# A plan's order settled twice, late from its end and early from its front, with new operation lengths, and expert lists worked out at another place

## The chip, the cores and the metric

One Trainium2 chip, one core of it. The metric is the device time of one execution in microseconds (us); where several executions were timed, the median is taken. TensorE (PE) does the matmuls, VectorE (DVE), ScalarE (ACT) and GpSimd (POOL) the elementwise work, and SyncE (SP) issues nearly all DMAs. Each engine works through its own queue of instructions in order, and semaphores hold an instruction until what it needs is there.

## The reference

For each of 4 batches, 49 agents attend to 11456 keys, the queries attend to the agents, and each of the resulting 45824 rows of 128 goes through one of 8 experts (two layers, 128 to 1024 to 128), the one with the greatest gate logit:

```
a2k = softmax(agents @ k.T * scale);  agent_v = a2k @ v
x   = softmax(q @ agents.T * scale) @ agent_v
logits = x @ w_gate;  e = argmax(logits);  gate = softmax(logits)[e]
out = gate * (relu(x @ w1[e]) @ w2[e])
```

## The kernel before

Products are done in 16-bit pairs (a high part and what is left over), so that one product becomes two or three matmuls.

**Stages of a batch.** A batch is 9 units of 10 blocks of 128 rows. `k_ops` loads the keys, splits them (ACT the high part, POOL the low part, line 352), makes scores on PE and keeps the running maximum. `v_ops` subtracts the maximum, exponentiates and sums with the values. `dense_ops` folds the agents' values into the first layer's weights of the batch's commonest expert (`Md`, `Mq`). `q_head` makes the queries' weights (`rows`), stores them and loads them turned (`et`); `quads` copies a part of it four times (`etq`). `q_tail` makes gate logits, and `gate_ops` makes the gate of two units at a time.

**Dense tiles.** Every row goes through the commonest expert. A unit is three tiles (4, 4 and 2 blocks). A group is two first-layer results `hp` (lines 1207 and 1216), their two parts `hhi` (ACT, line 1236) and `hlo` (DVE, line 1241), and the second layer into `yp` (lines 1224, 1225, 1230). There are 180 such groups. PSUM has three `hp` buffers, so the next group's first layer waits until an `hlo` has been read out of the buffer that it wants. In `group_ops` each group's second layer comes behind the next group's first layer, so the order of groups on PE is fixed.

**Lists and the other experts.** `r_ops` works out, mostly on DVE, which rows of a batch belong to other experts (lines 1004 to 1190, tiles `big`, `idx`, `ohx`): it needs all gates of the batch, and `min_loads` and `min_tile` (fetch the rows, run them through their expert, scatter the result over the dense one) need it. There are 8, 5, 0 and 1 such tiles for the four batches. `ready` says behind which unit of a later batch they begin.

**The planner.** Every step is an `Op` with an engine, an assumed cost, a key (its due place, counted in dense blocks), and the steps and buffers that it depends on. `Plan.run` goes forward in time. Of all steps whose inputs and buffers are there it takes the one that can start first (within `SLACK`, the one with the smaller key), and it looks no more than `WINDOW` = 20 blocks ahead of the first step left. Loads share one modelled DMA path of 300 GB/s. The moment a step is taken, its instructions are emitted; the order in which they are taken is the order of each engine's queue.

Of the kernel before, what the change touches and what calls it, by code (L numbers as in the profile page):

```python
# [19 lines left out]
P = 128  # L20
# [23 lines left out]
SLACK0, SLACK = 0.1, 0.08  # L44
AHEAD0 = 40.0


# [38 lines left out]
class Plan:  # L86
# [18 lines left out]
    def run(self, window):  # L105
# [51 lines left out]
        while left:  # L157
# [47 lines left out]
def agent_attention_moe(ctx: ExitStack, tc: tile.TileContext, qT, kT, v, agT, wg, w1, w2, out):  # L205
# [128 lines left out]
    def split(src, key, hk, pool=False, rings=("chi", "clo"), parts_=1, early=False, lowcost=0):  # L334
        st = Rec()
        n = UC // parts_
        gf = [Gen("wf" if parts_ > 1 else "cf") for _ in range(parts_)]
        gh, gl = Gen(rings[0]), Gen(rings[1])
        st.f, st.ld = [], []

        def hi():
            st.hi = part(rings[0])
            for i, f in enumerate(st.f):
                nc.scalar.copy(st.hi[:, i * n:(i + 1) * n], f)  # L344

# [15 lines left out]
        o2 = PL.op("POOL" if pool else "DVE", ((lowcost or pol(UC) + 0.2) if pool else dve(UC)), lo, hk, [o1], new=[gl], use=gf + [gh])  # L361
        return st, [o1, o2], [gh, gl]

    def scores(t, st, sp, gs, key, pair=False):
# [3 lines left out]
        def mm():  # L368
            p = r.p = new_hp()[:, 0:UA].rearrange("p (j a) -> p j a", a=A) if pair else misc([P, UB, A])
            for j in range(UB):  # L370
# [3 lines left out]
                nc.tensor.matmul(p[:, j], l, t.a[:, 0], start=False, stop=True)  # L374
        o = PL.op("PE", 0.92, mm, key, sp + [t.o_a], new=[gm], use=gs)
        return r, o, gm
# [99 lines left out]
    def v_ops(t, key, pool=()):  # L476
# [8 lines left out]
        for u in range(NU):  # L485
# [60 lines left out]
            if not one and u + 1 not in firsts:  # L546
                continue
            oM.append(PL.op("PE", 1.14 * len(run) + 0.1, mm, k, wait_ + oM[-1:], new=[] if one and u else [gv],
                            use=gfs + [t.gS] + ([gv] if one and u else [])))
# [157 lines left out]
    def dense_ops(t, key):  # L707
# [44 lines left out]
        for h in range(2):  # L752
# [97 lines left out]
    def q_head(t, u, k, pool=True, low=True):  # L850
# [49 lines left out]
        o1 = PL.op("ACT", act(UA), ex, k, [o], use=[gx])  # L900
        o2 = PL.op("ACT", 0.13 + act(UA), ehi, k, [o1], new=[grow], use=[gx])
        o3 = PL.op("POOL" if pool else "DVE", (pol(UA) + 0.1 if pool else dve(UA)) + 0.1, elo, k, [o2], use=[gx, grow])
        o4 = PL.op("POOL" if pool else "DVE", (pol if pool else dve)(UB * R1), again, k, [o2], use=[grow])
        U.o_ag = o4
# [3 lines left out]
        if not (t.b == 0 and u == 0):  # L908
            U.o_et = [PL.op("SP", 2.3, turn, k, [o5], new=[gt], nbytes=2 * UC * P)]
            return  # L910
# [38 lines left out]
    def gate_ops(t, u0, u1, k):  # L949
# [24 lines left out]
        c = n * NE * 0.00107  # L974
        o = PL.op("DVE", 0.7 + 3 * c, g1, k, [U.o_lg for U in t.U[u0:u1]], new=[g3, g4], use=[t.glg, t.gsm])
        t.o_lg.append(o)
        o = PL.op("ACT", act(n * NE), g2, k, [o], use=[g3])
        o = PL.op("DVE", 0.85 + c, g3_, k, [o, t.o_sig], use=[g3, g4, t.gsig, t.gisc])
        for U in t.U[u0:u1]:
# [4 lines left out]
    def r_ops(t, key):  # L984
# [269 lines left out]
    def group_ops(i, first, last, items, nbk, l1, cost, y, gyp, deps, use, wdeps, wuse, w):  # L1254
# [6 lines left out]
        for p in range(np_):  # L1261
            def f1(p=p):
                x[p].hp = new_hp()
                l1(p, [z.hp for z in x[:p + 1]])
            o1.append(PL.op("PE", cost[p], f1, i - 2.2 + 0.05 * p, deps[p] + before + o1[-1:], new=[g[p][0]],
                            use=use + [g[q][0] for q in range(p)]))
# [13 lines left out]
        for p in range(np_):  # L1280
            def l2a(p=p):
                if first and p == 0:
                    y.yp = new_yp()
                layer2_hi(y.yp, w(), x[p].hi, items[p], nbk, first and p == 0)
            new = [gyp] if first and p == 0 else []
            G.l2.append(PL.op("PE", 0.9 if p else 1.0, l2a, i + 0.1 * p, [o4[p]] + wdeps + G.l2[-1:], new=new,
                              use=[g[p][1]] + wuse + ([] if new else [gyp])))
        for p in range(np_):
            def l2b(p=p):
                layer2_lo(y.yp, w(), x[p].lo, items[p], nbk, last and p == np_ - 1)  # L1290
            G.l2.append(PL.op("PE", 0.45, l2b, i + 0.3 + 0.1 * p, [o3[p]] + G.l2[-1:], use=[g[p][2], gyp] + wuse))
        groups.append(G)
# [9 lines left out]
    def quads(i, t, u):  # L1302
# [4 lines left out]
        def go():  # L1307
            U.etq = buf("etq", [P, UC], U16)
            for r in range(4):
                nc.sync.dma_start(U.etq[32 * r:32 * r + RC], U.et[0:RC])  # L1310
        U.o_q = PL.op("SP", 2.4, go, max(U.key + 3, i - 12) if U.key > -900 else U.key + 1, U.o_et, new=[U.gq], use=[U.gt], nbytes=4 * R2 * UC * 2)
        if t.b == 0 and u == 0:
            U.o_q.after += t.o_ld

    def dense_tile(i, t, u, j0, nbk):
# [10 lines left out]
        for q in range(ng):  # L1326
# [9 lines left out]
            o = group_ops(i + 2 * q, q == 0, q == ng - 1, items, nbk, l1, (0.43, 0.96), y, gyp,  # L1336
                          (U.o_et + (t.o_Md[q:q + 1] if nbk == 4 else t.o_Md), [U.o_q] + (t.o_Mq[q:q + 1] if nbk == 4 else t.o_Mq)), [U.gt, U.gq, t.gMd, t.gMq], [t.o_Wd], [t.gWd], lambda: t.Wd)
# [20 lines left out]
        o = PL.op("ACT", act(n), yo, e + 0.05, [o], new=[gyo], use=[gyp])  # L1358
        o = PL.op("POOL", pol(n) + 0.05 * (nbk // 2 - 1), mul, e + 0.08, [o, U.o_gate], use=[gyo, t.gisc])
        stores[b].append(PL.op("SP", 0.6, store, e + 0.1, [o], use=[gyo], nbytes=nbk * 65536))  # L1360

# [11 lines left out]
    def build_ops(i, e, key):  # L1373
# [22 lines left out]
        o = PL.op("ACT", act(F), hi, key + 2, [o], new=[gs], use=[gf])  # L1396
        o = PL.op("POOL", pol(F) + 0.1, lo, key + 2, [o], use=[gf, gs])
        o_parts[i].append(dma(None, None, P * F * 4, key + 2, [o], use=[gs], fn=lambda: nc.sync.dma_start(parts[i][e], r.s)))
# [48 lines left out]
    def min_loads(t, key):  # L1447
# [9 lines left out]
        def ix():  # L1457
# [7 lines left out]
            nc.vector.memset(r.rt, BIG_ID)  # L1465
        o = PL.op("SP", 1.0, ld, key, [t.o_lst], new=[gl], nbytes=t.cap * P * 8)
        oi = PL.op("DVE", 0.75, ix, key + 1, [o], new=[gi, r.grt, Gen("fx")], use=[gl])
        for j in range(t.cap):
# [27 lines left out]
            k = key + 2 + 4 * j  # L1496
            o = PL.op("POOL", 1.3, info, k, [oi, t.o_info], use=[r.grt, gi], nbytes=2000)
            o = PL.op("POOL", 1.5, get, k, [o] + t.o_eb, new=[ger], use=[r.grt], nbytes=33000)
            o = PL.op("PE", 0.06, tr, k + 1, [o], new=[gp], use=[ger])
# [5 lines left out]
    def min_tile(i, t, j):  # L1505
# [5 lines left out]
        def ld():  # L1511
            c.v, c.w = stage(t, ds(j, 1))
        o = PL.op("SP", 1.6, ld, i - 10, [t.o_tab] + o_parts[0] + o_parts[1], new=[gv, gw], nbytes=P * F * 8)
        y = Rec()
        gyp = Gen("yp")
        op = group_ops(i, True, True, [ONE], 1, lambda p, hps: layer1(hps[0], c.v, x.xt), (1.34,), y, gyp,
                       ([x.o, o],), [x.gxt, gv], [o], [gw], lambda: c.w)
# [8 lines left out]
        op = PL.op("ACT", 0.37, yo, i + 0.05, [op], new=[gyo], use=[gyp, r.grt])  # L1526
        PL.op("POOL", 1.3, sc, i + 0.1, [op] + stores[t.b], nbytes=65536, use=[gyo, r.grt])

# [4 lines left out]
    wait = []  # L1533
    ready = {(1, 2, 0): 0, (2, 2, 0): 1, (3, 2, 0): 2, (3, 8, 8): 3}
    n = gap = 0
# [39 lines left out]
    for t in BT:  # L1575
        f = first[t.b]
        for u in range(1 if t.b == 0 else 0, NU):
# [106 lines left out]
```

## Time and profile before

| | us |
|---|---|
| median of 3 runs | 1013.07 (1012.22 to 1019.42) |
| the profiled execution | 1009.59 |
| its span, first to last instruction | 1007.8 |
| mean granted TensorE clock | 0.972 |

The profile shows one execution. A busy share is the time in which an engine had an instruction under way; what ended the idle time before an instruction is found from semaphores. Times in windows count from the span's start.

### The profile page before, as it was taken

How to read it: one execution, taken by the hardware profiler on the slowest of the kernel's cores; microseconds unless marked ns; L12 is line 12 of the kernel's file. 1: busy time of each engine (PE TensorE's matmuls, PEld its weight loads, DVE VectorE, ACT ScalarE, POOL GpSimd, SP SyncE). 2: the span in 40 equal slices, each digit the busy share in tenths (PEclk: the TensorE clock that was granted, in tenths of full speed). 3: DMA queues.
4: the chain of work that ended last, by engine and by line, in shares of the span. 5: the costliest groups of instructions: out<-in, count | busy, mean ns of one | idle time of the engine just before them, and what ended most of it. 6: DMA issues, size and time to landing. Idle time of an engine off the chain costs nothing. (4 is left out here: it accounts for less than half of the span.)

```text
span 1007.8 us, 34309 instructions
## 1 busy us (share of the span) xinstructions
PE 928.7 (92%) x14812; PEld 756.5 (75%) x14812; DVE 713.1 (71%) x1088; ACT 656.6 (65%) x891; POOL 505.1 (50%) x710
## 2 busy tenths in 40 slices
PE   4799999999899999999998998999999999999794
PEld 4667877877577788787877887888877778777574
DVE  7666677678976666655899766665788876767852
ACT  6467988867586777654676777755667666655352
POOL 4124988555495888242355578842225433311231
PEclk8799999999799999999999999999999999999898
DMA  9547699963696476566344926683344535231211
GB/s 339 198 123 242 224 277 244 293 243 124 195 282 206 153 206 162 141 215 173 104 138 132 295 80 173 190 249 105 104 122 117 128 96 162 77 75 48 66 28 31
DMA packets 156575, 165.33 MB, mean 164 GB/s; under 512 B 60190, under 2 KB 130075, under 8 KB 156414
## 3 DMA queue, kind: packets, MB, share of 16 engines
q1 hardware_dynamic: 155070, 162.11, 53.9%
q8 instruction: 118, 1.93, 0.8%
q0 software_dynamic: 1344, 0.93, 0.4%
q14 instruction: 43, 0.35, 0.1%
HBM read 98.65 MB, written 45.50 MB: 143 GB/s over the span
## 5 line engine op out<-in xcount | busy, mean ns | idle before, releaser
L1241 DVE SCALAR_TENSOR_TENSOR hlo<-hp,hhi 128x1024 f16<-128x1024 f32 x374 | 445.3, 1218 | 189.4 <-ACT hhi L1236 183.8
L1236 ACT ACTIVATE hhi<-hp 128x1024 f16<-128x1024 f32 x374 | 367.7, 1022 | 159.7 <-PE hp L1216 151.7
L1224 PE MATMUL yp<-Wd,hhi 128*128 128x128 f16 x2880 | 352.3, 222 | 1.0 <-ACT yo L1341 0.6
L1225 PE MATMUL yp<-Wd,hhi 128*128 128x128 f16 x2880 | 350.7, 221 | 0.6 <-issue 0.6
L1224 PEld LDWEIGHTS <-hhi 128*128 128x128 f16 x2992 | 292.1, 99 | 34.4 <-issue 30.9
L1225 PEld LDWEIGHTS <-hhi 128*128 128x128 f16 x2992 | 296.0, 99 | 2.8 <-issue 2.3
L1346 POOL TENSOR_TENSOR yo<-yo,isc 128x256 f32<-128x256 f32 x180 | 112.8, 644 | 244.8 <-ACT yo L1341 206.6
L352 POOL TENSOR_TENSOR clo<-cf,chi 128x512 f16<-128x512 f32 x186 | 185.7, 1028 | 79.3 <-ACT chi L344 58.1
L1207 PE MATMUL hp<-et,Md 128*128 128x512 f16 (+1 forms) x864 | 195.8, 347 | 28.3 <-DVE hlo L1241 27.7
L1230 PE MATMUL yp<-Wd,hlo 128*128 128x128 f16 x2880 | 193.0, 219 | 3.4 <-DVE hlo L1241 2.2
L1230 PEld LDWEIGHTS <-hlo 128*128 128x128 f16 x2992 | 175.5, 98 | 5.7 <-issue 2.6
L1207 PEld LDWEIGHTS <-Md 128*128 128x128 f16 x864 | 75.3, 98 | 67.0 <-issue 37.4
L1341 ACT COPY yo<-yp 128x512 f32<-128x512 f32 (+1 forms) x108 | 55.7, 516 | 71.8 <-PE yp L1230 48.7
L344 ACT CAST chi<-cf 128x1280 f16<-128x1280 f32 x62 | 78.1, 1263 | 12.7 <-DMA cf<-in_qT 6.6
L885 POOL TENSOR_TENSOR rows<-xs,rows 128x245 f16<-128x245 f32 x72 | 44.6, 641 | 81.9 <-ACT rows L880 81.6
L1216 PE MATMUL hp<-etq,Mq 19*128 19x512 f16 (+1 forms) x864 | 73.2, 355 | 0.0
L1216 PEld LDWEIGHTS <-Mq 19*128 19x128 f16 x864 | 18.9, 91 | 71.0 <-issue 70.9
L374 PEld LDWEIGHTS <-clo 128*128 128x128 f16 x670 | 54.3, 97 | 4.4 <-POOL clo L352 4.1
L372 PE MATMUL misc<-a,chi 128*128 128x49 f16 x630 | 56.5, 185 | 1.1 <-DVE xt L1439 0.4
L374 PE MATMUL misc<-a,clo 128*128 128x49 f16 x630 | 56.2, 185 | 0.9 <-POOL clo L352 0.9
L373 PE MATMUL misc<-a,chi 128*128 128x49 f16 x630 | 56.2, 186 | 0.0
L372 PEld LDWEIGHTS <-chi 128*128 128x128 f16 x630 | 50.9, 96 | 6.6 <-issue 4.2
(263 smaller groups left out, 1102.7 us busy)
## 6 DMA issues: line engine op xcount, KB each, us to landing
cf<-in_kT SPq DMA_DIRECT2D x36, 640.0 KB
cf<-in_v SPq DMA_DIRECT2D x35, 640.0 KB
cf<-in_qT SPq DMA_DIRECT2D x35, 640.0 KB
out<-yo SPq DMA_DIRECT2D x72, 256.0 KB
eb<-rows SPq DMA_DIRECT2D x36, 320.0 KB
wf<-in_w SPq DMA_DIRECT2D x16, 512.0 KB
etq<-et SPq DMA_DIRECT2D x144, 50.0 KB
vst<-parts SPq DMA_DIRECT2D x14, 512.0 KB
```

The source lines that it names most:

```text
L344: nc.scalar.copy(st.hi[:, i * n:(i + 1) * n], f)
L352: (nc.gpsimd if pool else nc.vector).tensor_tensor(st.lo[:, o], f[:, d], st.hi[:, o], op=OP.subtract)
L372: nc.tensor.matmul(p[:, j], h, t.a[:, 0], start=True, stop=False)
L374: nc.tensor.matmul(p[:, j], l, t.a[:, 0], start=False, stop=True)
L1207: nc.tensor.matmul(hp[:, c:c + n], m[:, fb * P:(fb + 1) * P], e, start=c % 512 == 0, stop=False)
L1216: nc.tensor.matmul(hp[:, c:c + n], m[r:r + R2, fb * P:(fb + 1) * P], e[r:r + R2], start=False, stop=(c + n) % 512 == 0)
L1224: nc.tensor.matmul(y, h, w[:, fb * 256 + P:(fb + 1) * 256], start=first and j == 0 and i == 0, stop=False)
L1225: nc.tensor.matmul(y, h, w[:, fb * 256:fb * 256 + P], start=False, stop=False)
L1230: nc.tensor.matmul(yp[:, j * P:(j + 1) * P], lo[:, c + j * P:c + (j + 1) * P], w[:, fb * 256:fb * 256 + P], start=False, stop=last and j = ...
L1236: nc.scalar.activation(hi, hp, AF.Relu)
L1241: nc.vector.scalar_tensor_tensor(lo, hp, 0.0, hi, op0=OP.max, op1=OP.subtract)
L1346: nc.gpsimd.tensor_tensor(v3[:, j:j + 2], v3[:, j:j + 2], t.isc[:, k0 + j:k0 + j + 2, 1:2].bitcast(F32).to_broadcast([P, 2, P]), op=OP.mult)
```

## The change

1. `Plan.run` still chooses an order step by step, but emits nothing. A new function `settle` takes that order. It makes edges from the dependencies and from the order in which ring buffers are given out. Then three times over it places all steps from the end backwards, each as late as its users and its engine allow, and then from the front, the steps with the earliest late start first, each at the earliest free place on its engine, gaps between steps placed before included. Steps are emitted by these start times. `settle` has no window and no slack, and a DMA's landing is bytes / 300 GB/s + 4 us for each one by itself.
2. About 30 assumed costs are set anew.
3. The due places of the lists of batches 0 to 2 are moved back, beside the next batch's dense tiles and the following batch's keys and values, and the minor tiles of batches 0 and 1 begin three units later.

```diff
-            o.fn()
             left -= 1
...
-        self.order = order
-        return max(o.fin for o in order)
+        self.order = self.settle(order)
+        for o in self.order:
+            o.fn()
+        return self.span
+
+    def settle(self, order):
...
+        def edge(d, i, begin=False):
+            if at[d] != i:
+                o = order[i]
+                lag = -d.cost if begin else d.nbytes / 300e3 + 4.0 + d.more + 0.0 if d.nbytes else 0.0 if d.eng == o.eng else d.lat + 0.05
+                pred[i].append((at[d], lag))
+                succ[at[d]].append((i, lag))
+
+        for i, o in enumerate(order):
+            for d in o.deps:
+                edge(d, i)
+            for d in o.after:
+                edge(d, i, True)
+            for g in o.new:
+                r = rings.setdefault(g.ring, [])
+                k = RINGS.get(g.ring, 1)
+                if len(r) >= k:
+                    for u in r[len(r) - k][1].users:
+                        edge(u, i)
+                if r:
+                    edge(r[-1][0], i, True)
+                r.append((o, g))
...
+        def early(key):
+            t, busy = [0.0] * n, {}
+            for i in turns(pred, succ, key):
+                o = order[i]
+                x = max([t[p] + order[p].cost + lag for p, lag in pred[i]], default=0.0)
+                L = busy.setdefault(o.eng, [])
+                j = bisect_right(L, (x, 1e9))
+                if j:
+                    x = max(x, L[j - 1][1])
+                while j < len(L) and x + o.cost > L[j][0] + 1e-9:
+                    x = max(x, L[j][1])
+                    j += 1
+                L.insert(j, (x, x + o.cost))
+                t[i] = x
+            return t
...
+        t = [o.fin - o.cost for o in order]
+        for _ in range(ROUNDS):
+            ends = [x + o.cost for x, o in zip(t, order)]
+            t = early(late(ends, max(ends)))
+        self.span = max(x + o.cost for x, o in zip(t, order))
+        return [order[i] for i in turns(pred, succ, t)]
...
-        t.o_an = PL.op("DVE", 0.9, c7, k, [o3], new=[t.gan, t.gbm], use=[gp, t.gav] + ([ga] if one else []))
+        t.o_an = PL.op("DVE", 1.4, c7, k, [o3], new=[t.gan, t.gbm], use=[gp, t.gav] + ([ga] if one else []))
...
-        t.o_em = PL.op("DVE", 0.35, e2, k if t.b else 8, [o])
+        t.o_em = PL.op("DVE", 1.1, e2, k if t.b else 8, [o])
...
-                t.o_Mq.append(PL.op("SP", 2.0, spread, k, [o2], new=new, use=use + [gl], nbytes=4 * R2 * 1024))
+                t.o_Mq.append(PL.op("SP", 3.05, spread, k, [o2], new=new, use=use + [gl], nbytes=4 * R2 * 1024))
...
-        o8 = PL.op("DVE", dve(n8), a8, k, [o7], new=[Gsf], use=[Gb])
+        o8 = PL.op("DVE", 1.5, a8, k, [o7], new=[Gsf], use=[Gb])
...
-            o10 = PL.op("DVE", 0.6, a10, k, [t.o_idx], new=[Ghl], use=[t.gidx])
+            o10 = PL.op("DVE", 1.4, a10, k, [t.o_idx], new=[Ghl], use=[t.gidx])
...
-        U.o_q = PL.op("SP", 2.4, go, max(U.key + 3, i - 12) if U.key > -900 else U.key + 1, U.o_et, new=[U.gq], use=[U.gt], nbytes=4 * R2 * UC * 2)
+        U.o_q = PL.op("SP", 3.15, go, max(U.key + 3, i - 12) if U.key > -900 else U.key + 1, U.o_et, new=[U.gq], use=[U.gt], nbytes=4 * R2 * UC * 2)
...
-    ready = {(1, 2, 0): 0, (2, 2, 0): 1, (3, 2, 0): 2, (3, 8, 8): 3}
+    ready = {(1, 5, 0): 0, (2, 5, 0): 1, (3, 2, 0): 2, (3, 8, 8): 3}
...
-                r_ops(t, Keys(k + 10, k + (42 if t.b < 3 else 22), 12))
+                r_ops(t, Keys(k + 10, k + 22, 12) if t.b == 3 else Keys(f + 92, f + 128, 12))
```

No instruction is added or removed; the order in each queue is what changes.

## Rows read from the trace of the kernel before

**Rows 1.** The page: busy time, share of the span and instructions of each engine.
```profile
PE 928.7 (92%) x14812; PEld 756.5 (75%) x14812; DVE 713.1 (71%) x1088; ACT 656.6 (65%) x891; POOL 505.1 (50%) x710
```

**Rows 2.** Windows: stretch, its length, each engine's busy time, granted clock, DMA share.
```profile
0.00:45.00 45.00, 25.97 (x484) 23.79 (x484) 29.19 (x65) 25.61 (x34) 11.44 (x24) 0.81 0.83 294
45.00:215.00 170.00, 162.69 (x2656) 131.34 (x2656) 118.25 (x187) 129.97 (x176) 110.74 (x153) 0.99 0.76 231
215.00:285.00 70.00, 60.37 (x814) 46.79 (x813) 59.60 (x90) 49.55 (x64) 40.23 (x44) 0.90 0.59 185
285.00:520.00 235.00, 226.26 (x3660) 186.07 (x3658) 160.46 (x236) 154.49 (x222) 136.61 (x195) 0.99 0.59 174
520.00:555.00 35.00, 30.82 (x479) 24.58 (x477) 33.89 (x51) 20.93 (x27) 19.28 (x24) 0.95 0.45 143
555.00:740.00 185.00, 180.45 (x2999) 149.61 (x2998) 122.42 (x190) 122.40 (x172) 103.50 (x154) 1.00 0.59 167
740.00:805.00 65.00, 62.42 (x977) 49.72 (x977) 56.10 (x86) 43.20 (x59) 27.65 (x37) 1.00 0.48 128
805.00:915.00 110.00, 108.70 (x1708) 87.39 (x1705) 75.79 (x104) 69.74 (x92) 35.02 (x54) 1.00 0.37 98
915.00:960.00 45.00, 37.15 (x522) 28.58 (x520) 37.72 (x62) 22.83 (x30) 10.66 (x14) 0.92 0.17 55
960.00:994.40 34.40, 33.88 (x534) 28.62 (x533) 19.62 (x24) 17.53 (x22) 8.93 (x15) 1.00 0.14 37
994.40:1007.80 13.40, 0.00 (x0) 0.00 (x0) 0.00 (x0) 0.37 (x1) 1.04 (x1) 0.65 0.06 15
```

**Rows 3.** Waits of PE: whole span, 215:285, 520:555, 915:960 (us, times, longest).
```profile
PE hp L1207 <- DVE hlo L1241: 27.7, 22, 4.9
...
PE hp L1207 <- DVE hlo L1241: 9.6, 5, 2.6
...
PE hp L1207 <- DVE hlo L1241: 4.2, 3, 3.5
...
PE hp L1207 <- DVE hlo L1241: 5.9, 2, 4.9
```

**Rows 4.** Timeline 262:272: start us, us, engine, line, operation, [idle before].
```profile
261.70 3.10 SPq L785 DMA_DIRECT2D Mq<-Ml  x4
...
262.26 1.57 DVE L1088 TENSOR_REDUCE sf<-big 128x90 f32<-128x720 f32 x1
...
264.68 0.21 DVE L1101 TENSOR_SCALAR idx<-idx 128x90 int32<-128x90 int32 x1
264.74 2.91 POOL L352 TENSOR_TENSOR clo<-cf,chi 128x512 f16<-128x512 f32 x3 [3.37 <-ACT chi L344]
264.80 1.16 DVE L1102 TENSOR_SCALAR idx<-idx 128x90 int32<-128x90 int32 x1
...
266.00 1.12 DVE L1103 CAST hl<-idx 128x180 f16<-128x180 int32 x1
...
267.05 1.21 DVE L1241 SCALAR_TENSOR_TENSOR hlo<-hp,hhi 128x1024 f16<-128x1024 f32 x1
...
268.31 1.01 PE L1207 MATMUL hp<-et,Md 128*128 128x512 f16 x2 [2.64 <-DVE hlo L1241]
```

**Rows 5.** Single lines: count, duration ns min/median/max, first and last start us.
```profile
L1004 DVE SCALAR_TENSOR_TENSOR big<-lg,em x4: 900/901/903, 212.9 to 916.9; 128x720 f32<-128x720 f32 x4
...
L1418 PE MATMUL misc<-ident,er x14: 216/219/258, 339.6 to 984.5; 128*98 128x128 f16 x14
...
L961 DVE TENSOR_TENSOR lg<-lg,gr x20: 235/261/4441, 82.1 to 914.2; 128x160 f32<-128x160 f32 x16, 128x80 f32<-128x80 f32 x4
```

**Rows 6.** Windows of tile big alone (columns as Rows 2, without POOL's), batches 1 and 2.
```profile
500.00:570.00 70.00, 0.00 (x0) 0.00 (x0) 10.96 (x12) 1.83 (x4) 0.98 0.55 172
747.00:805.00 58.00, 0.00 (x0) 0.00 (x0) 8.15 (x8) 1.86 (x4) 1.00 0.49 131
```

**Rows 7.** Windows of all work: 300:370, columns as Rows 2.
```profile
300.00:370.00 70.00, 65.89 (x1135) 53.30 (x1133) 42.80 (x60) 47.97 (x66) 51.84 (x69) 1.00 0.59 176
```

More of the change, by code (lines that the diff above doesn't have):

```diff
@@ L45 @@
 AHEAD0 = 40.0
+ROUNDS = 3
 CAP = (8, 5, 0, 1)
@@ L195, in run, with turns, late @@
                     push(u)
-        self.order = order
-        return max(o.fin for o in order)
+        self.order = self.settle(order)
[3 more added lines that the diff above has]
+    def settle(self, order):
+        from bisect import bisect_left, bisect_right
+        import heapq
+        n = len(order)
+        at = {o: i for i, o in enumerate(order)}
+        pred, succ = [[] for _ in order], [[] for _ in order]
+        rings = {}
+        def edge(d, i, begin=False):
[18 more added lines that the diff above has]
+                r.append((o, g))
+        def turns(links, back, key):
+            need = [len(x) for x in links]
+            h = [(key[i], i) for i in range(n) if not need[i]]
+            heapq.heapify(h)
+            while h:
+                _, i = heapq.heappop(h)
+                yield i
+                for j, _ in back[i]:
+                    need[j] -= 1
+                    if not need[j]:
+                        heapq.heappush(h, (key[j], j))
+        def early(key):
[13 more added lines that the diff above has]
+            return t
+        def late(key, end):
+            t, busy = [0.0] * n, {}
+            for i in turns(succ, pred, [-x for x in key]):
+                o = order[i]
+                x = min([t[s] - lag for s, lag in succ[i]], default=end)
+                L = busy.setdefault(o.eng, [])
+                j = bisect_left(L, (x, -1e9))
+                if j and L[j - 1][1] > x:
+                    j -= 1
+                    x = L[j][0]
+                while j and L[j - 1][1] > x - o.cost + 1e-9:
+                    j -= 1
+                    x = min(x, L[j][0])
+                L.insert(j, (x - o.cost, x))
+                t[i] = x - o.cost
+            return t
+        t = [o.fin - o.cost for o in order]
[4 more added lines that the diff above has]
+        return [order[i] for i in turns(pred, succ, t)]
@@ L360, in split @@
         o1 = PL.op("ACT", act(UC), hi, hk, st.ld, new=[gh], use=gf)
-        o2 = PL.op("POOL" if pool else "DVE", ((lowcost or pol(UC) + 0.2) if pool else dve(UC)), lo, hk, [o1], new=[gl], use=gf + [gh])
+        o2 = PL.op("POOL" if pool else "DVE", ((lowcost or pol(UC) + 0.45) if pool else dve(UC)), lo, hk, [o1], new=[gl], use=gf + [gh])
         return st, [o1, o2], [gh, gl]
@@ L374, in mm @@
                 nc.tensor.matmul(p[:, j], l, t.a[:, 0], start=False, stop=True)
-        o = PL.op("PE", 0.92, mm, key, sp + [t.o_a], new=[gm], use=gs)
+        o = PL.op("PE", 0.79, mm, key, sp + [t.o_a], new=[gm], use=gs)
         return r, o, gm
@@ L547, in v_ops @@
                 continue
-            oM.append(PL.op("PE", 1.14 * len(run) + 0.1, mm, k, wait_ + oM[-1:], new=[] if one and u else [gv],
+            oM.append(PL.op("PE", 1.08 * len(run) + 0.2, mm, k, wait_ + oM[-1:], new=[] if one and u else [gv],
                             use=gfs + [t.gS] + ([gv] if one and u else [])))
@@ L900, in q_head @@
         o1 = PL.op("ACT", act(UA), ex, k, [o], use=[gx])
-        o2 = PL.op("ACT", 0.13 + act(UA), ehi, k, [o1], new=[grow], use=[gx])
+        o2 = PL.op("ACT", 0.04 + act(UA), ehi, k, [o1], new=[grow], use=[gx])
         o3 = PL.op("POOL" if pool else "DVE", (pol(UA) + 0.1 if pool else dve(UA)) + 0.1, elo, k, [o2], use=[gx, grow])
-        o4 = PL.op("POOL" if pool else "DVE", (pol if pool else dve)(UB * R1), again, k, [o2], use=[grow])
+        o4 = PL.op("POOL" if pool else "DVE", 0.47 if pool else dve(UB * R1), again, k, [o2], use=[grow])
         U.o_ag = o4
@@ L908, in q_head @@
         if not (t.b == 0 and u == 0):
-            U.o_et = [PL.op("SP", 2.3, turn, k, [o5], new=[gt], nbytes=2 * UC * P)]
+            U.o_et = [PL.op("SP", 2.75, turn, k, [o5], new=[gt], nbytes=2 * UC * P)]
             return
@@ L974, in gate_ops @@
         c = n * NE * 0.00107
-        o = PL.op("DVE", 0.7 + 3 * c, g1, k, [U.o_lg for U in t.U[u0:u1]], new=[g3, g4], use=[t.glg, t.gsm])
+        o = PL.op("DVE", 0.95 + 3 * c, g1, k, [U.o_lg for U in t.U[u0:u1]], new=[g3, g4], use=[t.glg, t.gsm])
         t.o_lg.append(o)
         o = PL.op("ACT", act(n * NE), g2, k, [o], use=[g3])
-        o = PL.op("DVE", 0.85 + c, g3_, k, [o, t.o_sig], use=[g3, g4, t.gsig, t.gisc])
+        o = PL.op("DVE", 1.05 + c, g3_, k, [o, t.o_sig], use=[g3, g4, t.gsig, t.gisc])
         for U in t.U[u0:u1]:
@@ L1264, in f1 @@
                 l1(p, [z.hp for z in x[:p + 1]])
-            o1.append(PL.op("PE", cost[p], f1, i - 2.2 + 0.05 * p, deps[p] + before + o1[-1:], new=[g[p][0]],
+            o1.append(PL.op("PE", cost[p], f1, i - 2.2 + 0.05 * p, deps[p] + before + o1[-1:], lat=0.1 if p else 0.21, new=[g[p][0]],
                             use=use + [g[q][0] for q in range(p)]))
@@ L1285, in group_ops @@
             new = [gyp] if first and p == 0 else []
-            G.l2.append(PL.op("PE", 0.9 if p else 1.0, l2a, i + 0.1 * p, [o4[p]] + wdeps + G.l2[-1:], new=new,
+            G.l2.append(PL.op("PE", 0.89, l2a, i + 0.1 * p, [o4[p]] + wdeps + G.l2[-1:], new=new,
                               use=[g[p][1]] + wuse + ([] if new else [gyp])))
@@ L1290, in l2b @@
                 layer2_lo(y.yp, w(), x[p].lo, items[p], nbk, last and p == np_ - 1)
-            G.l2.append(PL.op("PE", 0.45, l2b, i + 0.3 + 0.1 * p, [o3[p]] + G.l2[-1:], use=[g[p][2], gyp] + wuse))
+            G.l2.append(PL.op("PE", 0.445, l2b, i + 0.3 + 0.1 * p, [o3[p]] + G.l2[-1:], use=[g[p][2], gyp] + wuse))
         groups.append(G)
@@ L1358, in dense_tile @@
         o = PL.op("ACT", act(n), yo, e + 0.05, [o], new=[gyo], use=[gyp])
-        o = PL.op("POOL", pol(n) + 0.05 * (nbk // 2 - 1), mul, e + 0.08, [o, U.o_gate], use=[gyo, t.gisc])
-        stores[b].append(PL.op("SP", 0.6, store, e + 0.1, [o], use=[gyo], nbytes=nbk * 65536))
+        o = PL.op("POOL", pol(n) + 0.15 * (nbk // 2 - 1), mul, e + 0.08, [o, U.o_gate], use=[gyo, t.gisc])
+        stores[b].append(PL.op("SP", 0.45, store, e + 0.1, [o], use=[gyo], nbytes=nbk * 65536))
     ok = "a count of seven comparisons"
@@ L1396, in build_ops @@
         o = PL.op("ACT", act(F), hi, key + 2, [o], new=[gs], use=[gf])
-        o = PL.op("POOL", pol(F) + 0.1, lo, key + 2, [o], use=[gf, gs])
+        o = PL.op("POOL", pol(F) + 0.25, lo, key + 2, [o], use=[gf, gs])
         o_parts[i].append(dma(None, None, P * F * 4, key + 2, [o], use=[gs], fn=lambda: nc.sync.dma_start(parts[i][e], r.s)))
@@ L1465, in ix @@
             nc.vector.memset(r.rt, BIG_ID)
-        o = PL.op("SP", 1.0, ld, key, [t.o_lst], new=[gl], nbytes=t.cap * P * 8)
+        o = PL.op("SP", 1.45, ld, key, [t.o_lst], new=[gl], nbytes=t.cap * P * 8)
         oi = PL.op("DVE", 0.75, ix, key + 1, [o], new=[gi, r.grt, Gen("fx")], use=[gl])
@@ L1496, in min_loads @@
             k = key + 2 + 4 * j
-            o = PL.op("POOL", 1.3, info, k, [oi, t.o_info], use=[r.grt, gi], nbytes=2000)
-            o = PL.op("POOL", 1.5, get, k, [o] + t.o_eb, new=[ger], use=[r.grt], nbytes=33000)
+            o = PL.op("POOL", 1.05, info, k, [oi, t.o_info], use=[r.grt, gi], nbytes=2000)
+            o = PL.op("POOL", 1.8, get, k, [o] + t.o_eb, new=[ger], use=[r.grt], nbytes=33000)
             o = PL.op("PE", 0.06, tr, k + 1, [o], new=[gp], use=[ger])
@@ L1512, in ld @@
             c.v, c.w = stage(t, ds(j, 1))
-        o = PL.op("SP", 1.6, ld, i - 10, [t.o_tab] + o_parts[0] + o_parts[1], new=[gv, gw], nbytes=P * F * 8)
+        o = PL.op("SP", 1.35, ld, i - 10, [t.o_tab] + o_parts[0] + o_parts[1], new=[gv, gw], nbytes=P * F * 8)
         y = Rec()
         gyp = Gen("yp")
-        op = group_ops(i, True, True, [ONE], 1, lambda p, hps: layer1(hps[0], c.v, x.xt), (1.34,), y, gyp,
+        op = group_ops(i, True, True, [ONE], 1, lambda p, hps: layer1(hps[0], c.v, x.xt), (1.335,), y, gyp,
                        ([x.o, o],), [x.gxt, gv], [o], [gw], lambda: c.w)
@@ L1526, in min_tile @@
         op = PL.op("ACT", 0.37, yo, i + 0.05, [op], new=[gyo], use=[gyp, r.grt])
-        PL.op("POOL", 1.3, sc, i + 0.1, [op] + stores[t.b], nbytes=65536, use=[gyo, r.grt])
+        PL.op("POOL", 2.6, sc, i + 0.1, [op] + stores[t.b], nbytes=65536, use=[gyo, r.grt])
     seq = []
```

2 lines of the change are left out of this document (1 added, 1 removed).

## The prediction

> **What bounds the kernel now.** First the page's busy times: PE is busy 928.7 us of 1007.8, no other engine above 71% [rows 1]. So the end is set by PE's work, and what an order can win is the time in which PE stands or runs slow. Where that is, the windows by stage show [rows 2]. From 45 to 994.4 us PE stands 46.7 us: 7.3, 9.6, 8.7, 4.2, 4.6, 2.6, 1.3, 7.9 and 0.5 us in the nine stretches, each the length less PE's busy time. The quiet stretch 805:915 shows that dense groups alone keep PE busy (1.3 us idle in 110). The granted clock is the second loss. It is 0.90 in 215:285, a mix of the levels 1.2 and 2.4 GHz, so up to 0.10 x 70 = 7.0 us of full-speed work is lost there; by the same product 1.7 us in 45:215, 2.4 in 285:520, 1.8 in 520:555 and 3.6 in 915:960, 16.4 us in all, an upper bound, since some of that time PE stood anyway.
>
> Next, who ends PE's waits: a first-layer matmul waiting for DVE's `hlo`, 27.7 us in 22 waits, the longest 4.9 [rows 3]. Of these 9.6, 4.2 and 5.9 us lie in 215:285, 520:555 and 915:960, and in those stretches, with 740:805, DVE is busiest: 85%, 97%, 84% and 86% [rows 2]. That is where the lists of batches 0, 1, 3 and 2 are worked out; the first step of the first one is at 212.9 us [rows 5]. The timeline shows how it comes about [rows 4]: from 262.26 to 267.05 DVE works through list steps (1.57, then small ones, then 1.16 and 1.12 us), and the `hlo` behind them begins at 267.05 and ends at 268.26. PE stood 2.64 us for it. The old planner thought these steps short: 0.89 us for L1088 (1.57 in the trace), and 0.6 for the four of `a10` (0.21 for L1101, 1.16 and 1.12 for two others). And it takes whatever can start first, so a long list step slips in ahead of an `hlo` that becomes ready a moment later.
>
> **The change part by part.** *New costs.* They lie nearer to the trace: `a8` 1.5 for 1.57, `a10` 1.4 for a sum that was over 2.4 in this place, `spread` 3.05 for four issues that take 3.10 us [rows 4]. By themselves they cost nothing; they make the plan's gaps true ones.
>
> *The settled order.* A step that is due late is placed after those due early, and only in a gap that it fits. The `hlo` of the next group is due at once. The list of batch 0 isn't due until its rows are fetched; their first matmul was at 339.6 us [rows 5], and with minor tiles three units later it is some 30 blocks later. A block takes (994.4 - 45) / 374 = 2.54 us (360 dense blocks and 14 minor tiles), so that is about 76 us more. From 213 to 416 us DVE was busy 59.6 us in the first 70 and 68% after that [rows 2]: (59.6 + 0.68 x 131) / 201 = 74%, the list included. There is room for it in gaps. The list of batch 3 feeds one tile at the very end, whose first matmul is at 984.5 [rows 5], so it needn't hold up groups in 915:960 either. On PE itself the order of groups is fixed by edges; only small steps between them move.
>
> I take back about two thirds of the loss where lists stand before `hlo`: 12 of 16.6 us (9.6 idle, 7.0 clock) in 215:285, 4 of 6.0 in 520:555, 2 of 2.6 in 740:805, 8 of 11.5 in 915:960. In the other five stretches 22.4 us of idle and 4.1 of clock are spread over many causes; I take 9 of 26.5. Sum 35. The bounds: nothing, and 46.7 + 16.4 = 63.1 us.
>
> *Lists moved beside keys and values.* There POOL has more to do: 51.84 of 70 us in 300:370 [rows 7] against 40.23 of 70 in 215:285 [rows 2]. The trace shows that some DVE steps grow while POOL works. L1102 and L1101 have one shape; the one that began with POOL idle took 0.21 us, the other, with three POOL splits under way, 1.16 [rows 4]. L961 has a median of 0.261 and a longest of 4.441 us [rows 5]. The `hlo` isn't touched: 1.21 us in the same place [rows 4]. The list steps on `big` took 10.96 us in batch 1, where POOL was 55% busy (19.28 of 35), and 8.15 in batch 2, where it was 43% (27.65 of 65) [rows 2, 6]. That is 2.8 us for 12 points. At 74%, 19 points more, it comes to some 4 us more for each of batches 0 and 1, 8 us of DVE; not all of it holds PE, and I take 4. The bounds are 0 (the steps fall into gaps) and 12 (half as much again, all of it in front of an `hlo`).
>
> The Trainium skill has a rule on this: the page "SBUF — State Buffer", section "SBUF: two separate sides", says that VectorE and GpSimd share one pair of ports as an exclusive lock, taken for a whole instruction by whichever comes first. It fits L1102 and L961, and it speaks against a list beside POOL's splits; by it alone the change would lose in each batch's list. What that would give is the first rival below.
>
> *DMAs.* SP's queue is reordered too. `settle` lets every load land by itself, while 0:45 shows the DMA share at 0.83 and 294 GB/s [rows 2], so the start is where its picture is least true. The order of loads through each buffer ring is kept, which holds most of it in place. From the rows: one foreign load of 0.66 MB ahead of the keys costs 0.66 / 294 GB/s = 2.2 us; two would be 4.4, and as much might be gained by closing some of the 19 us that PE stands there. I take 0, from -5 to +5. The tail, 994.4 to 1007.8 [rows 2], stays.
>
> **The sum.** 1009.6 us (profiled execution: 1007.8 of span and 1.8 around it) - 35 + 4 = 978.6. The median of the runs lies 3.5 us above the profiled execution, so I forecast 982 us.
>
> **The rivals.** *The stall moves with the list.* By the lock, list steps grow behind POOL, overrun their gaps, and the `hlo` behind them comes late again, at 280 to 420 us. For it: L961 at 4.4 us. Against: DVE at 74% there, and the list cut into gaps. Price: of the 26 us counted for list stretches only half comes, and the port costs its 12: 35 - 13 - 12 = 10 us, so 1003.
>
> *Nothing much changes.* The groups' order on PE is fixed, and the 22.4 us outside list stretches come from causes that an order can't mend; the gaps in the plan are thinner than its errors. Against: 27.7 of 46.7 us wait for one DVE step that stands behind steps not yet due. Time 1003 to 1023.
>
> *Slower: DMAs land late.* Without the shared path and the window, the plan puts issues where modelled landings just suffice; in full stretches (share 0.76 over 45:215 [rows 2]) they come later, and SP's queue holds the turned rows and the quads behind an issue that waits. Each of 36 units has one quad; `settle` counts 3.15 us to issue it and 4 to land. If each quad came late by t, PE would lose 36 t: at 31 / 36 = 0.9 us the whole gain is gone, at 1.7 us the time is 1013 - 31 + 61 = 1043. For it: that share. Against: before, none of PE's waits in the view of rows 3 was ended by a DMA, and the new plan issues as early as the rings allow.
>
> **How the numbers follow.** About 1% is what a measurement of this kernel can tell from no change: under 1003 is faster, over 1023 slower. The forecast (965 to 998) has 0.56; a better one, where three quarters of the 63 us or more come back (950 to 965), 0.10; the stall that moves 0.10, two thirds of it under 1003; no change 0.10; late DMAs 0.14. Faster: 0.56 + 0.10 + 0.07 = 0.73; same 0.03 + 0.10 = 0.13; slower 0.14. Eight in ten lie between 958 and 1013: about 0.04 below, and the late DMAs with the upper edge of no change above.
>
> **What would show it.** Right: PE's waits for `hlo` fall from 27.7 to under 12 us, the longest under 2; PE's idle time from 45 us to the end of its work from 46.7 to about 20; the clock is at 1.00 in nearly all stretches; list steps stand one or two at a time between `hlo`; DVE, POOL and ACT busy times are the same within some us. Wrong: PE waits for `et`, `etq` or `Mq` by DMA (the third rival), `hlo` waits reappear at 280 to 420 us with long list steps (the first), the first 45 us grow, or PE's busy time itself grows.

## The result and the profile after

The changed kernel took 999.63 us (median of 4 runs, 996.85 to 1001.96), the kernel before beside it 1015.88. The ratio is 0.985 (95% interval 0.981 to 0.989): about 16 us faster, where 31 were forecast. The time lies within the eight-in-ten bounds (958 to 1013) but just above the forecast's own band (965 to 998), and the gain is half of what was said.

The profiled execution of after spans 999.9 us. Its page, engine busy times (before in [rows 1]):

```profile
PE 928.2 (93%) x14812; PEld 758.4 (76%) x14812; DVE 720.9 (72%) x1088; ACT 656.2 (66%) x891; POOL 506.8 (51%) x710
```

PE is busy as long as before, DVE 8 us longer. Where PE stands, the windows of after show (columns as in [rows 2]):

```profile
125.00:150.00 25.00, 19.47 (x327) 15.81 (x325) 18.54 (x28) 17.74 (x25) 21.49 (x31) 0.86 0.63 184
150.00:215.00 65.00, 64.26 (x1036) 53.03 (x1033) 43.49 (x64) 51.85 (x70) 45.24 (x68) 1.00 0.93 275
215.00:310.00 95.00, 95.00 (x1490) 76.57 (x1487) 70.11 (x106) 75.17 (x98) 51.71 (x66) 1.00 0.70 215
310.00:330.00 20.00, 15.96 (x286) 13.14 (x284) 17.89 (x22) 14.47 (x19) 16.35 (x18) 0.96 0.48 146
330.00:360.00 30.00, 24.71 (x431) 19.56 (x431) 28.43 (x38) 19.68 (x26) 15.29 (x22) 0.91 0.53 155
360.00:450.00 90.00, 84.49 (x1332) 70.08 (x1332) 61.48 (x87) 55.79 (x82) 65.92 (x93) 0.98 0.57 167
525.00:550.00 25.00, 20.76 (x314) 16.21 (x311) 20.44 (x33) 14.21 (x24) 16.22 (x22) 0.80 0.66 196
915.00:950.00 35.00, 27.64 (x385) 20.88 (x383) 27.51 (x43) 16.87 (x21) 7.28 (x9) 0.90 0.10 27
```

The stretch 215:310, where the first list stood before, has no idle PE left at all. But 310:450 has 14.8 us of it (4.0, 5.3 and 5.5), and up to 0.04 x 20 + 0.09 x 30 + 0.02 x 90 = 5.3 us of slow clock. DVE is at 93% from 310 to 360 (17.89 + 28.43 of 50). PE's waits, first over the whole span, then in 310:430, say for whom:

```profile
PE hp L1292 <- DVE hlo L1326: 19.5, 15, 4.9
...
PE hp L1292 <- DVE hlo L1326: 10.2, 4, 4.9
```

It is the `hlo` again (line 1326 of after answers to 1241). Half of what is left of that wait is now where the list of batch 0 went. The timeline there, DVE's rows with one of POOL and one of PE:

```profile
322.44 0.59 DVE L1146 COPY q<-big 128x8 f32<-128x8 f32 x1
...
324.54 5.74 POOL L437 TENSOR_TENSOR clo<-cf,chi 128x512 f16<-128x512 f32 x6
...
324.63 1.08 DVE L1151 TENSOR_SCALAR qi<-qi 128x8 int32<-128x8 int32 x1
325.75 1.08 DVE L1156 CAST q<-qi 128x8 f32<-128x8 int32 x1
...
327.49 1.07 DVE L1158 TENSOR_TENSOR q<-q 128x8 f32<-128x8 f32 x1
...
329.59 1.21 DVE L1326 SCALAR_TENSOR_TENSOR hlo<-hp,hhi 128x1024 f16<-128x1024 f32 x1
...
330.86 1.01 PE L1292 MATMUL hp<-et,Md 128*128 128x512 f16 x2 [4.89 <-DVE hlo L1326]
...
346.20 1.20 DVE L1187 TENSOR_SCALAR idx<-idx 128x90 int32<-128x90 int32 x1
```

Ten steps on at most 8 numbers a partition (`a5` and `a5b`, planned at 1.6 us together) run from 322.44 to 329.67, 7.2 us, while POOL works without a break, from 324.54 on at low parts. Of the ten, nine end when a POOL instruction ends (the tenth, which fills a single number, takes 0.06 us): POOL's pieces of 512 columns take 1.15 us here, and the steps beside them 1.07 or 1.08. The `hlo` behind the ten begins at 329.59, and PE has stood 4.9 us for it. The index steps (`a9`, `a10`) took 5.4 us at 343 against 2.07 planned.

The list was not in the gaps from 213 us on. Its first step and its first matmuls in after (columns as in [rows 5]):

```profile
L1089 DVE SCALAR_TENSOR_TENSOR big<-lg,em x4: 884/900/902, 223.4 to 911.5; 128x720 f32<-128x720 f32 x4
...
L1116 PE MATMUL misc<-oh,ones x8: 312/316/327, 281.1 to 917.6; 128*128 128x360 f16 x8
```

It began at 223.4, but the first of its four counting matmuls ran at 281.1, the other three from 311.9 on, and the DVE steps behind them from 315.5 on. These matmuls write to `misc`, of which there is one buffer, and `settle` keeps the order in which the first pass gave that buffer out, an order that follows the due places to within the 20 blocks of the window. That this order held the list back is read from the code and these times; no run changed it alone, and PE, which had no idle time from 215 to 310 us, may have had its part in it.

### The profile page after: what moved, and what is told of

The parts are those of the page before. It is cut to its first block, busy times and chain, and to the rows that moved or that the text cites. A ratio compares the mean times of both kernels' runs of the same rounds, so it can differ in the third digit from the quotient of the medians.

```text
span 999.9 us, 34355 instructions
## 1 busy us (share of the span) xinstructions
PE 928.2 (93%) x14812; PEld 758.4 (76%) x14812; DVE 720.9 (72%) x1088; ACT 656.2 (66%) x891; POOL 506.8 (51%) x710
## 4 chain that ended last, share of the span: by engine, by line
PE 47%; issue 5%; DVE 4%; POOL 3%; ACT 1%; DMA 1%; POOLq 0%; SPq 0%; DVEq 0%; ACTq 0%
PE yp L1309 10%; PE yp L1315 9%; PE yp L1310 9%; PE hp L1292 9%; PE hp L1301 3%; PE misc L605 2%; DVE hlo L1326 2%; POOL clo L437 1%; POOL yo L1431 1%; ACT hhi L1321 1%; PE misc L459 1%; PE misc L457 1%; PE misc L1236 1%; PE misc L458 1%; PE misc L1019 0%
## 5 line engine op out<-in xcount | busy, mean ns | idle before, releaser
L1292 PE MATMUL hp<-et,Md 128*128 128x512 f16 (+1 forms) x864 | 194.2, 347 | 20.0 <-DVE hlo L1326 19.5
```

The lines of the kernel that those rows point to most:

```text
L1292: nc.tensor.matmul(hp[:, c:c + n], m[:, fb * P:(fb + 1) * P], e, start=c % 512 == 0, stop=False)
```

## The experiments

Each was timed in 5 rounds (e6 in 3) against the kernel before on its own chip. They ran in four groups of four, e1 to e4 and so on, each group on one chip. The kernel before took 1010.4, 1009.7, 1017.6 and 1007.3 us in the four, so medians are compared inside a group; between groups a ratio tells more, but not to 0.5%.

**Which part does what: e1, e2, e3.** e1 is the kernel before with `settle` and nothing else of the change. e2 is the full change with the old places. e3 is the full change without `settle`, with `Plan.run` as before. The edit of e2, and the line that e3 takes back:

```diff
-    ready = {(1, 5, 0): 0, (2, 5, 0): 1, (3, 2, 0): 2, (3, 8, 8): 3}
+    ready = {(1, 2, 0): 0, (2, 2, 0): 1, (3, 2, 0): 2, (3, 8, 8): 3}
-                r_ops(t, Keys(k + 10, k + 22, 12) if t.b == 3 else Keys(f + 92, f + 128, 12))
+                r_ops(t, Keys(k + 10, k + (42 if t.b < 3 else 22), 12))
...
-        self.order = self.settle(order)
+        self.order = order
```

> The settled order alone, with the old costs and the old places of lists and minor tiles. Theory A (the new order wins only as far as the assumed lengths are true): 1003 to 1012 us, waits of PE for hlo above 20 us, since list steps are still planned too short. Rival B (the priority of hlo over list steps is what wins, whatever the lengths): 994 to 1002 us, as the full change.

> The settled order with the new costs, but lists and minor tiles at their old places (the first list some 90 us earlier, where POOL has fewer low parts to make). Theory A (lists moved beside POOL's low parts give the gain back, because DVE's list steps wait for POOL's instructions): 986 to 996 us, faster than the full change by 4 us or more, and the ten small list steps that took 7.2 us at 322 to 330 us take under 4. Rival B (the new place helps, the loss is elsewhere): 1000 to 1008 us.

> The new costs and the new places, but the old forward order without settling. Theory A (settling is the part that wins, costs and places alone little): 1006 to 1016 us with waits of PE for hlo at 20 us or more. Rival B (true lengths are most of it): 995 to 1003 us.

Measured: e1 986.4 us, ratio 0.976 (0.974 to 0.979). e2 985.8, 0.975 (0.972 to 0.978). e3 1008.1, 0.999 (0.997 to 1.002). So settling wins some 24 us by itself, the new lengths add nothing that can be told, and costs and places without settling win nothing. Rival B of e1 had the reason right, though its time is some 8 us too long. The `hlo` waits are 17.9 us in e1 and 15.5 in e3, where theory A of each asked for 20 or more. And the settled order with both places as before beats the full change by about 1%: the third part of the change takes back some of what the first won.

**Which of the two places: e5.** The lists at their old place, the minor tiles three units later as in the change.

```diff
-                r_ops(t, Keys(k + 10, k + 22, 12) if t.b == 3 else Keys(f + 92, f + 128, 12))
+                r_ops(t, Keys(k + 10, k + (42 if t.b < 3 else 22), 12))
```

> The settled order and new costs, minor tiles three units later as in the full change, but the lists' due places as before. Tells which of the two moves costs. Theory A (the lists' place costs, by POOL's splits): about as with both old places, 982 to 990 us. Rival B (later minor tiles cost, for instance by meeting the next batch's work): 995 to 1002 us.

Measured: 984.9 us, 0.977 (0.974 to 0.979), as e2. It is the lists. DVE's timeline of e5, three of the same small steps:

```profile
247.99 1.08 DVE L1148 COPY q<-q 128x7 f32<-128x7 f32 x1
...
249.51 0.17 DVE L1151 TENSOR_SCALAR qi<-qi 128x8 int32<-128x8 int32 x1
249.72 0.17 DVE L1156 CAST q<-qi 128x8 f32<-128x8 int32 x1
```

Three windows of e5 (columns as in [rows 2]):

```profile
100.00:150.00 50.00, 44.94 (x837) 37.09 (x834) 35.39 (x46) 41.47 (x54) 44.15 (x58) 0.90 0.64 193
215.00:285.00 70.00, 63.91 (x959) 50.02 (x956) 63.15 (x104) 55.64 (x72) 42.16 (x44) 1.00 0.69 219
895.00:940.00 45.00, 37.64 (x551) 29.25 (x549) 35.86 (x55) 21.57 (x28) 10.37 (x13) 0.92 0.10 30
```

Here one of the ten steps met a POOL instruction (1.08), the others took 0.25 or less; the ten took 2.8 us. The stretch 215:285, with the list in it, has 6.1 us of idle PE and a clock of 1.00, for 9.6 and 0.90 before [rows 2].

**Is it POOL's work: e4, e15, e11.** The order of steps stays; POOL fills with zeros where it subtracted. e4 and e15 are the same edit on the full change, e11 is it on e5.

```diff
         def lo():
             st.lo = part(rings[1])
+            if pool and not early:
+                nc.gpsimd.memset(st.lo, 0.0)
+                return
```

> The full change in the same order of steps, but POOL fills the low parts of later keys and of queries with zeros instead of subtracting (that part of the scores is left out), so that POOL reads nothing from SBUF there and is done sooner. Theory A (list and gate steps on DVE wait for POOL's instructions, and the plan has no room for that): 984 to 992 us; the list steps at 322 to 330 us shrink from 7.2 us to under 3.5, the wait of 4.9 us near 326 us goes; the wait of 4.9 us near 927 us, where POOL is idle, stays. Rival B (DVE is planned so full there that PE waits anyway, or loads are late): 996 to 1002 us, the wait near 326 us stays above 3 us.

> As the old-place lists with later minor tiles (settled, new costs), but POOL fills the low parts of later keys and of queries with zeros (that part of the scores is left out). Theory A (at the old place POOL's splits cost the lists little, 2.8 us for ten small steps that take 2.2 to 2.6 with POOL idle): at most 3 us faster than with the splits, 980 to 985 us, so the 10 us that the same edit won at the new place belong to the place. Rival B (the splits slow the whole kernel, wherever the lists are): 8 us or more faster, 973 to 978 us.

Measured: e4 985.8 us, 0.976 (0.973 to 0.980), a ratio lower than the full change's by some 9 us. e11 985.2 us, 0.968 (0.966 to 0.971). Its ratio is lower than e5's, but the kernel before was slower on that chip (1017.6 us against 1009.7); the median is e5's within 0.3 us, and e10, which has the splits and differs by an edit worth about 1 us (below), took 985.1 beside it. So at the old place POOL's splits cost nothing that shows, and at the new one they cost about the whole loss. The last group sets this side by side on one chip (e13 is e5 again, e14 the full change, e15 is e4):

> Settled, new costs, later minor tiles, lists at their old places. Theory A (the place is nearly all of the 16 us): 12 us or more below e14 on this chip. Rival B (a good part of it was the last list's yielding): 6 to 10 us below e14.

> The full change, as the measure for the other three of this call. Both theories: ratio to the kernel before 0.982 to 0.988.

> The full change, with POOL filling the low parts of later keys and of queries with zeros (that part of the scores is left out). Theory A (at the new place the lists lose by waiting for POOL's instructions): as e13 within 3 us. Rival B (DVE is too full there whatever POOL does): half the distance or less between e14 and e13 is won back.

Measured: lists old (e13) 986.5 us, 0.978 (0.974 to 0.982); lists new (e14, the full change) 997.1, 0.989 (0.986 to 0.993); lists new, no splits (e15) 986.2, 0.979 (0.975 to 0.982). The place costs 10.6 us, between the two expectations of e13, and leaving the splits out wins 10.9 back. DVE's time goes the same way: summed over the rows of `r_ops` and `tiles_of` in each trace, the lists of batches 0 and 1 took 46.9 us of DVE in e13, 59.2 in e14 and 48.7 in e15. At the new place that is 12.3 us more of DVE, for the 10.6 of time. e9, the full change in the third group, took 1001.0 us, 0.984 (0.982 to 0.987).

> The full change once more, beside the others of this call on the same chip, so that the places of the lists are compared on one chip. Theory A (the new place of the lists costs about 8 us): 996 to 1002 us, at least 6 us above e10. Rival B (the difference between the calls was one of chips): within 3 us of e10.

DVE's timeline of e4 at the new place, with POOL's fills:

```profile
321.68 2.54 DVE L1154 TENSOR_SCALAR qi<-qi 128x8 int32<-128x8 int32 x1
321.93 2.27 POOL L434 MEMSET clo<- 128x1280 f16 x2
...
324.26 0.17 DVE L1159 CAST q<-qi 128x8 f32<-128x8 int32 x1
...
340.96 0.25 DVE L1191 CAST hl<-idx 128x180 f16<-128x180 int32 x1
```

The index steps are down from 5.4 to 1.5 us. The ten small steps still took 5.7, 2.54 of them behind two fills: against the expectation the fills hold DVE too, and the wait near 327 us fell only from 4.9 to 3.4. So the time is theory A's and this sign is rival B's; the win isn't that one wait alone, since over all their steps the lists of batches 0 and 1 took 48.6 us of DVE in e4, about as in e15. POOL was busy 21.13 us of 50 in 310:360, against 31.64 in after.

**Do the true lengths help: e12.** The plan is told what the list steps of batch 0 took in after, and the same lengths for batch 1, where they were too long: there the ten steps took 2.4 us of the 7.2 told and the index steps 1.9 of 5.3.

```diff
-        o5 = PL.op("DVE", 0.9, a5, k, [o3], new=[Gq], use=[Gb])
+        o5 = PL.op("DVE", 3.6 if t.b < 2 else 0.9, a5, k, [o3], new=[Gq], use=[Gb])
-        o5 = PL.op("DVE", 0.7, a5b, k, [o5], new=[Goff], use=[Gq])
+        o5 = PL.op("DVE", 3.6 if t.b < 2 else 0.7, a5b, k, [o5], new=[Goff], use=[Gq])
...
```

`a9` goes from 0.67 to 1.9 in the same way, `a10` from 1.4 to 3.4.

> The full change with the lists of batches 0 and 1 at the new place, but the plan is told the lengths that they have there (3.6 and 3.6 us for the two groups of small steps, 1.9 and 3.4 us for the index steps, instead of 0.9, 0.7, 0.67 and 1.4). Theory A (the place itself costs: the list steps fill DVE there, and knowing their length only moves the wait into the plan): 994 to 1003 us. Rival B (only the wrong lengths cost, a plan that knows them puts hlo first): 984 to 991 us, waits of PE for hlo between 310 and 430 us under 3 us in all.

Measured: 1002.5 us, 0.985 (0.982 to 0.988), no better than e9 beside it. PE's waits in 310:430 of e12:

```profile
PE hp L1292 <- DVE hlo L1326: 5.6, 4, 3.4
PE misc L457 <- DVE xs L957: 2.8, 1, 2.8
```

The `hlo` waits there fell from 10.2 to 5.6 us, and others came up. In the new order the lengths were other ones again: batch 0's index steps took 1.6 us, batch 1's ten steps 4.2 us of DVE, and the lists of both batches 58.1 us of DVE, against 59.2 in e9. Lengths fixed ahead bought nothing; a plan that works out a step's length where it puts it was not tried.

**Shorter POOL instructions: e7.** The pieces of a low part are cut to 256 columns.

```diff
-                for c in range(0, n, 4 * P) if pool else (0,):
+                for c in range(0, n, 2 * P) if pool else (0,):
```

> The full change, its order unchanged, but POOL's low parts are cut into pieces of 256 columns instead of 512 (ten short instructions for five, about 0.55 us instead of 1.03 each, some 0.3 to 0.5 us more in all for one unit). Theory A (each small DVE step waits for the POOL instruction under way): the ten list steps at 322 to 330 us fall from 7.2 us to 4 to 5, and the time to 992 to 998 us. Rival B (it is POOL's total share that counts, or another cause): the ten steps stay above 6 us and the time stays at 998 to 1004 us.

Measured: 996.5 us, 0.987 (0.985 to 0.989). The count in the expectation was wrong: a low part was three pieces (512, 512, 256) and became five. Line 437 in e7 (columns as in [rows 5]):

```profile
L437 POOL TENSOR_TENSOR clo<-cf,chi x310: 657/671/2025, 46.1 to 854.2; 128x256 f16<-128x256 f32 x155
```

And two of the ten steps in DVE's timeline of e7:

```profile
322.72 0.34 DVE L1151 TENSOR_SCALAR qi<-qi 128x8 int32<-128x8 int32 x1
323.09 0.59 DVE L1156 CAST q<-qi 128x8 f32<-128x8 int32 x1
```

The piece of 256 takes 0.67 us. The steps that took 1.07 or 1.08 take 0.34 to 0.59, the ten 4.9 us instead of 7.2: theory A's mechanism. On the time it is inconclusive, within the error of the full change: the lists of batches 0 and 1 still took 56.2 us of DVE, 3 less than in e14, and POOL works 22.5 us longer in all (529.3 against 506.8).

**The last list: e6, e16, e8.** In e2 PE waits 4.9 us for an `hlo` near 918 us, as in after near 932. e6 (from e2) and e16 (from after) let the last batch's list steps count as due 6 us later; e8 (from e2) makes its query units due sooner.

The first hunk is that of e6 and e16, where `o.soft` is 6.0 for DVE steps of the last batch's `r_ops` and otherwise 0; the second that of e8.

```diff
-            t = early(late(ends, max(ends)))
+            t = early([x + o.soft for x, o in zip(late(ends, max(ends)), order)])
...
-                k = f - LEAD + 8 * u
+                k = f - LEAD + 7 * u
```

> Old places, settled, new costs, but when placing from the front the last batch's list steps on DVE count as due 6 us later than the backward pass says, so that hlo steps of that time are placed first. Theory A (that list heads a chain of fetch, tile and scatter that is as long as the work left, so its early place is right and only trades one wait for another): 986 to 994 us, no faster than without, PE's wait near 913 us smaller and PE idle behind 950 us larger. Rival B (the list has room; the wait of 4.9 us is lost for nothing): 979 to 983 us.

> The full change, with the last batch's list steps yielding 6 us to hlo. Theory A (yielding trades one wait for another): within 3 us of e14. Rival B: 5 us or more below e14.

> Old places, settled, new costs, and the last batch's query units due 7 blocks apart instead of 8, so that its list can begin sooner and isn't pressed against the end. Theory A (the wait of 4.9 us for hlo near 913 us comes from that list's urgency): 977 to 983 us, the longest wait for hlo behind 850 us under 3 us. Rival B (the same steps stand in front of the same kind of hlo, only sooner): 983 to 989 us and a wait of 4 us or more some 10 to 20 us sooner.

Measured: e6 984.9 us, 0.974 (0.971 to 0.977), between the two expectations and 0.001 under e2. e16 996.0, 1.1 us below e14. e8 985.2, 0.977 (0.974 to 0.980). The longest waits for `hlo` near the end, in e2 behind 895 us:

```profile
PE hp L1292 <- DVE hlo L1326: 4.9, 1, 4.9
```

In e6 behind 895 us (its line numbers are 3 higher):

```profile
PE yp L1318 <- DVE hlo L1329: 2.3, 2, 1.5
```

In e8 behind 880 us:

```profile
PE hp L1292 <- DVE hlo L1326: 7.5, 1, 7.5
```

Yielding takes the 4.9 us wait away, but the time moves by 1 us in both trials: from 895 us to the end of its work PE stood 6.3 us in e6 and 8.0 in e2, since shorter waits came in place of the long one. With the list sooner the wait only comes sooner, and is longer (rival B of e8). In after the last list's scan began at 919.9 us and the scatter that needs the list was issued at 990.7, while PE works until 987.3: what hangs on the list takes as long as the rest of PE's work. The backward pass may therefore put it ahead of `hlo`; no run took that chain apart, and the last thing that the scatter waited for was a store of dense rows (4.23 us), not the list.

**Together: e10.** e5 with the last list yielding.

> Settled, new costs, minor tiles three units later, lists at their old places, and the last batch's list steps yielding 6 us to hlo. Theory A (each of these was as fast as or a little faster than the rest): 980 to 986 us. Rival B (the yielding list ends later than the work that hides it): 987 to 992 us with PE idle at the end.

Measured: 985.1 us, 0.968 (0.965 to 0.970), 16 us below e9 beside it: faster than both kernels.

## Why the prediction was wrong where it was

**What bounds the kernel: right.** The waits for `hlo` behind list steps were the lever: where a list step stands in front of one, after shows the same picture as [rows 4].

**The settled order: right in kind, too large.** I took 35 us; e1, e2, e5 and e13 give 21 to 25 with the lists where they were. In time this is the larger miss, 10 us or more. The mechanism holds: in e13 PE waited 11.9 us for `hlo`, before 27.7 [rows 3]. By stretch, in e5: 215:285 lost 6.1 us where 16.6 were lost [rows 2], so 10.5 came of 12. The last list gave nothing of 8: 895:940 still lost 7.4 us of idle and up to 0.08 x 45 = 3.6 of clock. And a stretch that I counted as a gain became a loss: 100:150 has 5.1 us of idle and up to 5.0 of clock in e5; before, that stretch lost 2.1 us (window of the kernel before):

```profile
100.00:150.00 50.00, 47.86 (x898) 39.07 (x896) 35.71 (x49) 44.37 (x57) 46.73 (x61) 1.00 0.82 259
```

In e5's timeline a gate step takes 2.83 us there; before, as L961, it took 0.26 in the median and 4.44 at its longest [rows 5]:

```profile
129.67 2.83 DVE L1046 TENSOR_TENSOR lg<-lg,gr 128x160 f32<-128x160 f32 x1
```

And PE waits for a step that stands behind it on DVE (waits of PE in e5, 100:150):

```profile
PE misc L457 <- DVE mx L523: 2.9, 1, 2.9
```

e1, with the old costs, doesn't have this wait and is no faster over all: it stands 0.4 us in 100:150, but 5.8 in 45:100 and 3.8 in 150:215, where e2 stands 5.4, 2.4 and 0.0. So from 45 to 215 us, where I counted on a gain, the new order only moved the loss (7.3 us before [rows 2]).

**The lists' new place: the term whose working failed.** I put 4 us, bounds 0 to 12; on one chip it is 10.6. With this term as forecast and the settled order's as measured the gain would have been about 20 us (24 - 4), the other way round about 24 (35 - 10.6). Three steps of the argument were wrong. First, that the list would be spread over gaps from 213 to 416 us at a DVE load of 74%: most of it ran after 312, held back, as the code has it, by the order of the `misc` buffer, and from 310 to 360 DVE was at 93%. Second, the price itself: I read 2.8 us for 12 points of POOL's share out of 10.96 us on `big` in batch 1 and 8.15 in batch 2 [rows 6], but these are 12 steps and 8. Batch 2 has no minor tiles, and the four steps that it lacks are most of the 2.8 us (rows of tile `big` before, batch 1):

```profile
L1191 DVE TENSOR_SCALAR big<-jiota,tm x1: 906/906/906, 547.7 to 547.7; 1x5 f32<-1x5 f32 x1
L1192 DVE TENSOR_TENSOR big<-big,end x1: 620/620/620, 548.6 to 548.6; 1x35 f32<-1x35 f32 x1
L1193 DVE TENSOR_REDUCE big<-big x1: 203/203/203, 549.3 to 549.3; 1x5 f32<-1x35 f32 x1
L1194 DVE CAST tab<-big x1: 158/158/158, 549.5 to 549.5; 1x5 int32<-1x5 f32 x1
```

The eight steps that both batches have took 9.1 and 8.2 us, 0.9 apart, which by the same working makes 3 us of DVE and not 8. That the 8 came as near as it did to the 12.3 measured is luck. It is the small steps that grew most: in batch 0 ten steps from 0.17 to as much as 1.08 us each, 4.4 us more than at the old place, and 3.9 us more for the index steps, both groups in front of an `hlo` that PE waited for. Third, I let half of DVE's growth hold PE; for 12.3 us of it the time lost 10.6. That this would be the stall which moves with the list was the first rival; it stood at 1003 with a chance of 0.10, and its place (280 to 420 us) and cause are what the runs show, together with a forecast mechanism that worked.

The Trainium skill's page "SBUF — State Buffer", section "SBUF: two separate sides", that spoke against the change, agrees with the traces of after and e7: the step waits out POOL's whole instruction (1.07 or 1.08 us beside pieces of 512 columns, 0.58 or 0.59 beside pieces of 256). What it makes of the time was weighed at 4 us and is 10.6.

**New lengths at no cost: right** (e1 against e2, 0.6 us). **DMAs: right**: of PE's waits in after 2.1 us in all were ended by one. **The signs:** the `hlo` waits fell to 19.5 us, not under 12, and reappeared at 280 to 420, which was named as the sign of the first rival. PE's idle time from 45 us to the end of its work is 41.6 us, where about 20 were forecast and 46.7 stood before; the clock is below 1.00 in six of the eight stretches above; PE's busy time didn't grow.

## What to carry to other kernels

Placing work that isn't due for long into gaps was worth more here than better lengths: 24 us against nothing that could be told. But a buffer with one slot can carry the old due places into the new order, so look at the steps that use it (here the `misc` matmuls) before believing that others are free to move. Before moving VectorE work beside GpSimd work, count its instructions, not its microseconds: each one of the kinds that grew here cost up to a GpSimd instruction more. The `hlo` steps did not (1.21 us), so look at the rows of each kind. And before taking a price from two totals, see that they count the same steps.

## What was not expected of the hardware

A DVE step on 8 numbers a partition took 0.17 us or up to 1.08, by the POOL instruction under way. A POOL fill, which reads nothing, held one too, and one step can wait through more than one POOL instruction: 2.54 us until the second of two fills of together 2.27 ended (e4). A POOL piece of 256 columns takes 0.67 us, where one of 512 takes 1.15 (after, 324 to 330 us).

Left open: why the full change lies 16 us above e10 on one chip, where the lists' place (10.6) and the yielding (1.1) add up to 12 on another; and which links of the last list's chain make it as urgent as the backward pass has it.
